# Sigmoid attention and GELU feed-forward: the seven Strassen parts of each w_out block group formed and stored in one go

## Chip, core and metric

One NeuronCore of a Trainium2 chip runs the whole program. The metric is the device time of one execution in microseconds (us). Before the change the median of three runs is 1015.89 us, from 1015.17 to 1016.56.

## What is computed

```python
scale = 1.0 / np.sqrt(q.shape[-1])
scores = scale * np.matmul(q, k.transpose(0, 1, 3, 2)) - np.log(S)
attn_out = np.matmul(1.0 / (1.0 + np.exp(-scores)), v)
x = attn_out.transpose(0, 2, 1, 3).reshape(B * S, H * D)
h = x @ w_in
g = 0.5 * h * (1.0 + erf(h / sqrt(2)))
out = g @ w_out
```

There are 8 batches of 12 heads with 448 positions of 64, so x is 3584 x 768; w_in is 768 x 2048 and w_out is 2048 x 768, both 64-bit floats.

## The kernel before

The program has two stages. **Attention** (24 units of two heads, to 242.7 us of the trace) writes x, partly into tiles and mostly to DRAM (scr_x). The **feed-forward** then runs over four blocks of two batches. Each block has a first product with w_in (`ffn1`, 56 steps) and a second with w_out (`ffn2`, 28 steps). Both use a Strassen-Winograd scheme: instead of eight block products there are seven, and the weights enter as seven parts, numbered 1 to 7. With the blocks a11, a12, a21, a22 of a weight the parts are: 1 = a11, 2 = a12, 4 = a22, 5 = s1 = a21 + a22, 6 = s2 = s1 - a11, 7 = s3 = a11 - a21, 3 = s4 = a12 - s2.

Every product is three matmuls (`terms`, L579): each operand is split in a high and a low half, and low x high, high x low and high x high are added up. So each weight tile needs a copy on ACT (the high half, `high_to`, L302) and a subtraction on DVE (the low half, `low_to`, L313), in this order.

**Weights for the feed-forward.** The class `Weights` loads tiles wst0, wst1, ... from DRAM through the SP queue, four buffers in all; ACT and DVE split tile k into whl k, again four buffers. Call this *unit k*. A unit of `ffn1` feeds two steps: unit k feeds steps 2k and 2k+1 of the list `IN_ORDER`. A step is nine matmuls of 448 columns. wst k+4 is asked for when the low half of unit k is done; the copy of unit k+4 waits until PE has used unit k. `IN_ORDER` has steps 0 to 15 for parts 1 and 2, steps 16 to 39 for parts 6, 7 and 4, the rest for 5 and 3. Part 7 goes on in the PSUM bank of part 6, and part 4 in that of part 7, so ACT must first copy out what the earlier part left: step 18 waits for the copy of step 16 (L732), step 20 for that of step 17, and step 21 (part 4) for that of step 18 (L734).

**The decoder.** The weights come as 64-bit floats. `Decoder.work` (L224) is a generator that turns them into 32-bit ones, in 28 chunks (16 of w_in, 12 of w_out): a load of about 1 MB by SP (`load`, raw, three buffers), two ACT instructions (`scale`, `place`, tile me), three DVE instructions (`join` L171 and L179, `round` L186), and then the load of the chunk three later. Two chunks make a *group*, four blocks of 128 x 512 in one tile wd (two buffers). w_out has six groups, 0 to 5. For each group the seven parts are stored to DRAM (scr_out) by DMAs that POOL issues, 256 KB each, and read back as weights later. The steps of the generator are spread over the attention units by a table and over the steps 2 to 45 of the first `ffn1` by `to`. All instructions stand on each engine in the order in which Python writes them; no scheduler moves them.

**How a group ends before the change.** `post` (L205 on) makes s1 in place of a21 (L209) and s2 (L210) in a small tile s, and stores parts 2, 4, 1, 5, 6. Some steps later `close` (L217) makes parts 3 and 7 *in place* of a12 and a22: 3 = a12 - s2 and 7 = a22 - s2 (both L220; apart from rounding the second is a11 - a21). These two must wait until the stores of a12 and a22 have read them, and only when the last two stores have landed is the wd tile free for the group two later. Group 0 gets its first part at the end of the attention, with s2 in a buffer of the ring tmp, which also holds the attention's results on their way to scr_x:

```python
            if u == total - 1:
                dec.second = lambda group: piece("s2_0")
...
                    if dec.closed < min(KE + 1, len(opened)) and n >= opened[dec.closed] + (5 if n > 3 else 3):
                        dec.close()
```

Of the kernel before, what the change touches and what calls it, by code (L numbers as in the profile page):

```python
# [8 lines left out]
F32 = mybir.dt.float32  # L9
# [6 lines left out]
ALU = mybir.AluOpType  # L16

P = 128
# [4 lines left out]
def tile_sigmoid_attention_gelu_ffn(  # L23
# [10 lines left out]
    nc = tc.nc  # L34
    B, NPAIR, _, S = q.shape
    NU = NPAIR // 2
    D = HALF
    NF, _, NC, _ = w_in.shape
# [74 lines left out]
    def piece(name):  # L113
        return sb.tile([P, QUAD], F32, tag="tmp", name=name, bufs=3)

    def square(m):
        return m.rearrange("p (h f n) -> p h f n", h=2, f=2)

    class Decoder:
        def __init__(self):  # L120
            self.raws, self.parts, self.rest, self.out = {}, {}, {}, None
            self.done = self.groups = self.closed = 0
            self.mixing, self.pending, self.open, self.second = [], [], [], None
            self.steps = self.work()
            self.taken = 0

# [64 lines left out]
            self.load(i + 3)  # L191

        def post(self):
            some = bool(self.mixing or self.pending and self.second)
            while self.mixing:
                j, a = self.mixing.pop()
                s = sb.tile([P, 2, WU], F32R, tag="whl", name=f"sin{j}", bufs=WHL)
                s = s.bitcast(F32).rearrange("p a b -> p (a b)")
                quads = [t[:, i * OP : i * OP + OP] for t in (a, s) for i in range(4)]
                parts = mix(quads[:4], quads[4:])  # L200
                for p in (1, 2, 4, 5, 6, 7, 3):
                    n = IN_ORDER.index((p, j))
                    nc.gpsimd.dma_start(scr_in[n // 2][:, n % 2], parts[p])
                self.done += 1
            while self.pending and self.second:  # L205
                (c, e), a = self.pending.pop(0)
                a11, a12, a21, a22 = (a[:, i * QUAD : i * QUAD + QUAD] for i in range(4))
                s2 = self.second(c * KE + e)
                nc.vector.tensor_tensor(a21, a21, a22, op=ALU.add)  # L209
                nc.vector.tensor_tensor(s2, a21, a11, op=ALU.subtract)  # L210
                for p, part in ((2, a12), (4, a22), (1, a11), (5, a21), (6, s2)):
                    nc.gpsimd.dma_start(scr_out[p, c][:, :, :, e], square(part))
                self.open.append((c, e, a12, a22, s2))
                self.groups += 1
            return some

        def close(self):  # L217
            c, e, a12, a22, s2 = self.open.pop(0)
            for p, part in ((3, a12), (7, a22)):
                nc.vector.tensor_tensor(part, part, s2, op=ALU.subtract)  # L220
                nc.gpsimd.dma_start(scr_out[p, c][:, :, :, e], square(part))
            self.closed += 1

        def work(self):  # L224
            for i in range(3):
                self.load(i)
            yield
            for i in range(len(CHUNKS)):
                self.scale(i)
                yield True  # L230
                self.place(i)
                yield True
                yield self.post()
                self.join(i)
                yield True
                self.round(i)
                yield True
            yield self.post()

        def go(self, steps):  # L240
            for _ in range(steps):
# [7 lines left out]
                    steps += 1  # L249

        def has(self, *need):
            return all(n >= m for n, m in zip((self.done, self.groups, self.closed), need))

        def until(self, *need):
            while not self.has(*need):
# [4 lines left out]
    LATE = 17  # L260
    STEPS = {u: (3, 2) for u in (*range(2, 10), *range(11, 19))}
    STEPS |= {20: (3, 1), 21: (4, 1), 22: (4, 1), 23: (4, 0)}
    STEPS_IN_ALL = 5 * len(CHUNKS) + 2

    class Weights:
        def __init__(self):
# [7 lines left out]
        def need(self, i):  # L274
            kind, b, u = self.units[i]
            if b > 0:
                return 0, 0, 0
            if kind == "in":
                return max(j for _, j in IN_ORDER[2 * u : 2 * u + 2]) + 1, 0, 0
            groups = KE if u[1] < KF // 4 else 2 * KE  # L280
            return KF, groups, groups if u[0] in (3, 7) else 0

        def source(self, i):
            kind, b, u = self.units[i]
# [60 lines left out]
        nc.vector.tensor_tensor(lo, src, hi, op=ALU.subtract)  # L345

    def ring(name, tag="raw"):
        n, bufs = {"raw": (RAW, 3), "me": (KC * S, 2), "wd": (4 * QUAD, 2), "s": (KC * S, 1)}[tag]
        return (late if tag == "s" else sb).tile([P, n], F32R, tag=tag, name=name, bufs=bufs)

    def braid(m):
# [12 lines left out]
    def attention(at, ps):  # L364
# [153 lines left out]
        def decode(u, place):  # L518
            if u >= total:
                return  # L520
            if u == total - 1:
                dec.second = lambda group: piece("s2_0")
            dec.go(STEPS.get(u, (0, 0))[place])

        ready = nc.const_aps.tensor(1.0, (P, S), mybir.dt.bfloat16)
# [60 lines left out]
    def feed_forward(banks):  # L586
# [110 lines left out]
        def ffn1(b, g, xs):  # L697
# [6 lines left out]
                    held[p, j] = bank()  # L704
                    nc.scalar.copy(held[p, j], g[1, 0][j // 2][:, j % 2])

            done, opened = dec.taken, []
            live = [n for n in range(2, 46) if IN_ORDER[n] not in X0_WORK]
            for n, (p, j) in enumerate(IN_ORDER):
                if n % 2 == 0:  # L710
# [38 lines left out]
                if b == 0:  # L749
                    if at in X0_WORK:  # L750
                        X0_WORK[at](xs)
                    if n in live:
                        share = (live.index(n) + 1) / len(live)
                        dec.to(math.ceil(done + (STEPS_IN_ALL - done) * share))
                    while len(opened) < dec.groups:
                        opened.append(n)
                    if dec.closed < min(KE + 1, len(opened)) and n >= opened[dec.closed] + (5 if n > 3 else 3):
                        dec.close()
                else:
                    sums = {(1, 0): 5, (1, 1): 6, (1, 2): 7, (1, 4): 4}  # L760
                    highs = {(1, 3): 6, (1, 5): 7, (1, 7): 4, (6, 3): 5, (7, 7): 3}
                    lows = {(1, 4): 6, (1, 6): 7, (2, 6): 4, (6, 4): 5, (4, 7): 3}
                    if at in sums:
                        x_sum(xs, b, sums[at])
                    if at in highs:
                        x_high(xs, b, highs[at])
                    if at in lows:
                        x_low(xs, lows[at])
# [7 lines left out]
        def ffn2(b, g):  # L776
# [19 lines left out]
            for n, (p, c) in enumerate(OUT_ORDER):  # L796
# [53 lines left out]
                if p == 6:  # L850
                    after = c == KF // 2 - 1
                    sum21 = lambda g21=g21, g12=g12: combine(g21, g21, g12)
                    later.append(sum21) if after else sum21()
                if b == 0 and n in (0, 2):
                    dec.close()
                if b + 1 < NB and n == (4 if b else 8):
                    for p, j, k in ((1, 0, 0), (8, 0, 1), (3, 1, 1), (2, 1, 0)):
                        nxt[p] = x_tile("xs", f"x{b + 1}_{j}{k}")
                        load_x(nxt[p], b + 1, j, k)
            return nxt  # L860

        def second(group):
            if group not in seconds:
                s = late.tile([P, KC * S], F32, tag="s", name=f"s2_{group}", bufs=1)
                parts = (s[:, :QUAD], s[:, QUAD : 2 * QUAD])
                seconds.update({group: parts[0], group + 1: parts[1]} if group > KE else {group: s[:, :QUAD]})
            return seconds[group]

        seconds = {}
        dec.second = second  # L870
        h2, t4 = (x_tile(f"xt{i}", f"x0_{i}") for i in range(2))
        nc.scalar.copy(h2, x0[1, 0].bitcast(F32))
        nc.scalar.activation(one, one, AF.Gelu)
# [48 lines left out]
```

## Time and profile before

| what | value |
|---|---|
| median of three runs | 1015.89 us (1015.17 to 1016.56) |
| the profiled execution, its own time | 1015.95 us |
| its span, first to last instruction | 1013.9 us |
| mean granted TensorE clock | 0.999 |
| PE busy | 1005.8 us (99%) |
| DVE busy, ACT busy, POOL busy | 704.5, 679.4, 116.1 us |
| moved by DMA | 201.22 MB |

PE is the TensorE matmul engine, DVE VectorE, ACT ScalarE, POOL GpSimd, SP the engine that issues most DMAs; "SPq" is its DMA queue. A row of the timeline gives start, duration, engine, line, operation, what it writes and reads, and in square brackets the idle time of the engine just before with what ended it. "DMA to landing" is the time from the issue of a DMA until its data are there. The profiled execution lies 0.06 us above the median.

### The profile page before, as it was taken

The numbers are of one execution on the slowest core, as the hardware profiler recorded it, in microseconds if no ns is written. First come the engines' busy times: TensorE is split into PE (matmuls) and PEld (weight loads), VectorE is DVE, ScalarE is ACT, GpSimd is POOL, SyncE is SP. The second block draws the span as 40 slices with busy tenths as digits, with TensorE's granted clock in tenths as the row PEclk, the third lists the DMA queues.
The fourth block names the chain that finished last, engine by engine and source line by source line (L and its number), as shares of the span: only waits on it lengthen the run. The fifth ranks groups of instructions, "written<-read, shape, count | busy, mean of one in ns | idle before, by whom it ended". The sixth has DMA issues, their size and how long they took to land.

```text
span 1013.9 us, 16551 instructions
## 1 busy us (share of the span) xinstructions
PE 1005.8 (99%) x6406; PEld 908.2 (90%) x6406; DVE 704.5 (69%) x822; ACT 679.4 (67%) x935; POOL 116.1 (11%) x186
## 2 busy tenths in 40 slices
PE   9999999999999999999999999999999999999998
PEld 5656666566999999999999999999999999999998
DVE  3677767787788997774378867534887774368873
ACT  5888887788887656467665655766666567665652
POOL 1342223232322210010000000100000000000000
PEclk9999999999999999999999999999999999999999
DMA  9999999997996674564344445634445543334441
GB/s 271 294 352 354 306 334 322 352 337 249 317 334 225 200 245 149 165 205 137 115 130 133 145 141 165 203 124 121 136 113 143 163 153 118 110 109 125 143 141 59
DMA packets 84141, 201.22 MB, mean 198 GB/s; under 512 B 9760, under 2 KB 34336, under 8 KB 84064
## 3 DMA queue, kind: packets, MB, share of 16 engines
q1 hardware_dynamic: 71056, 158.53, 51.2%
q0 software_dynamic: 12704, 41.30, 11.3%
q8 instruction: 50, 0.82, 0.3%
q10 hardware_dynamic: 304, 0.34, 0.1%
q14 instruction: 27, 0.22, 0.1%
HBM read 156.10 MB, written 41.29 MB: 195 GB/s over the span
## 4 chain that ended last, share of the span: by engine, by line
PE 83%; issue 8%; DMA 5%; DVE 2%; POOL 1%; ACT 1%; SPq 0%; POOLq 0%; DVEq 0%; ACTq 0%
PE pf L584 72%; PE pav L470 6%; PE sc L437 4%; DMA scr_x<-x 2%; DMA scr_in<-wd 1%; PE sc_t L454 1%; POOL scr_x L516 1%; DMA scr_out<-wd 1%; DMA wst<-scr_in 1%; DVE wd L171 1%; DVE whl L316 0%; PE warm L529 0%; ACT a L415 0%; DVE xl_p L621 0%; DMA out_dram<-tmp 0%
## 5 line engine op out<-in xcount | busy, mean ns | idle before, releaser
L584 PE MATMUL pf<-op,whl 128*128 128x448 f32 x2016 | 382.0, 352 | 0.0
L584 PEld LDWEIGHTS pf<-op,whl 128*128 128x128 f32 x2016 | 381.0, 189 | 0.3
L584 PE MATMUL pf<-xh_p,whl 128*128 128x448 f32 x1296 | 353.3, 353 | 1.5 <-ACT g L732 1.5
L309 ACT CAST whl<-wst 128x768 fp32r<-128x768 f32 x224 | 186.5, 833 | 212.9 <-PE pf L584 186.5
L316 DVE TENSOR_TENSOR whl<-wst,whl 128x768 fp32r<-128x768 f32 x224 | 213.7, 955 | 145.5 <-ACT whl L309 145.2
L584 PEld LDWEIGHTS pf<-xh_p,whl 128*128 128x128 f32 x1296 | 244.9, 189 | 3.3 <-ACT g L732 1.8
L584 PE MATMUL pf<-xl_p,whl 128*128 128x448 f32 x600 | 211.6, 353 | 1.5 <-DVE xl_p L621 1.5
L415 ACT ACTIVATE a<-sc 128x896 f32<-128x896 f32 x144 | 119.2, 935 | 35.6 <-PE sc L437 35.5
L470 PE MATMUL pav<-a,v 64*64 64x448 f32 x1296 | 133.0, 541 | 0.0
L621 DVE TENSOR_TENSOR op<-g,op 128x896 fp32r<-128x896 f32 x112 | 121.4, 1084 | 0.9 <-ACT op L631 0.9
L584 PEld LDWEIGHTS pf<-xl_p,whl 128*128 128x128 f32 x600 | 113.4, 189 | 1.9 <-DVE xl_p L621 1.8
L470 PEld LDWEIGHTS pav<-a,v 64*64 64x64 f32 x1296 | 55.4, 132 | 61.1 <-issue 33.7
L631 ACT CAST op<-g 128x896 fp32r<-128x896 f32 x112 | 104.8, 936 | 2.6 <-PE pf L584 2.6
L621 DVE TENSOR_TENSOR g<-g,g 128x896 f32<-128x896 f32 x64 | 69.4, 1084 | 0.0
L618 ACT ACTIVATE g<-tmp 128x448 f32<-128x448 f32 x64 | 40.4, 631 | 26.7 <-DVE tmp L621 26.6
L621 DVE TENSOR_TENSOR tmp<-pf,g 128x448 f32<-128x448 f32 x64 | 39.8, 623 | 26.2 <-PE pf L584 25.6
L341 POOL DMA_DIRECT2D x<-scr_x x24 | 18.0, 807 | 325.3 <-ACT g L728 219.3
L437 PE MATMUL sc<-lo,hi 64*128 64x448 f32 x276 | 51.5, 368 | 0.3 <-DVE x L508 0.3
L407 DVE TENSOR_TENSOR lo<-qk,hi 128x896 fp32r<-128x896 f32 x46 | 50.1, 1089 | 1.1
L437 PE MATMUL sc<-hi,lo 64*128 64x448 f32 x276 | 48.9, 349 | 0.0
L437 PE MATMUL sc<-hi 64*128 64x448 f32 x276 | 48.9, 349 | 0.0
L171 DVE SCALAR_TENSOR_TENSOR wd<-raw,me 128x768 uint32<-128x768 uint32 (+1 forms) x28 | 30.0, 1072 | 20.6 <-ACT me L152 11.3
(74 smaller groups left out, 773.1 us busy)
## 6 DMA issues: line engine op xcount, KB each, us to landing
wst<-scr_in SPq DMA_DIRECT2D x112, 384.0 KB, 3.2
wst<-scr_out SPq DMA_DIRECT2D x112, 384.0 KB, 3.1
v<-v_dram SPq DMA_DIRECT2D x48, 256.0 KB, 8.6
raw<-w_in_dram SPq DMA_DIRECT2D x16, 767.8 KB, 7.2
raw<-w_out_dram SPq DMA_DIRECT2D x12, 1023.5 KB, 7.8
qk<-q_dram SPq DMA_DIRECT2D x23, 448.0 KB, 10.9
qk<-k_dram SPq DMA_DIRECT2D x46, 224.0 KB, 11.4
out_dram<-tmp SPq DMA_DIRECT2D x43, 224.0 KB, 2.1
```

The costliest lines, as they stand in the source:

```text
L171: nc.vector.scalar_tensor_tensor(bits, words, 13, self.parts.pop(i), op0=ALU.logical_shift_right, op1=ALU.bitwise_or,)
L309: nc.scalar.copy(hl[:, 0], t)
L316: nc.vector.tensor_tensor(hl[:, 1], t, hl[:, 0], op=ALU.subtract)
L341: queue.dma_start(dst[:, :, a], src[:, :, a])
L407: nc.vector.tensor_tensor(lo, raw, hi, op=ALU.subtract)
L415: nc.scalar.activation(to, sc, AF.Sigmoid, bias=NEG_LOG_S, scale=SCALE)
L437: nc.tensor.matmul(sc[:, j], ks[rows(j), 1, keys], braid(qs[rows(j), 0]) if braided else qs[rows(j), 0], start=n == 0, stop=n == last,)
L470: nc.tensor.matmul(pav[rows(j), p], vals[u][half, p, j, c], a[p][half, j], start=not swap and c == order[0], stop=c == (order[-1], FULL - ...
L584: nc.tensor.matmul(bank, a, braid(m), **flags)
L618: nc.scalar.activation(straight(dst), unbraid(src), AF.Gelu)
L621: nc.vector.tensor_tensor(out, a, b, op=op)
L631: nc.scalar.copy(op[:, 0], src)
```

## The change

The two parts that were made in place, and s2, go to a tile of their own, s, with three pieces of 128 x 512 and one buffer. `post` now makes s3 (in s) and s1 (in place of a21, the only block that is still overwritten, and before it is stored) and issues the stores of parts 1, 2, 4, 5 and 7. A new step, `rest_of_group`, makes s2 and s4 in s and stores parts 6 and 3. `close`, the lists of open groups and the calls of `close` in `ffn1` and `ffn2` are gone. The tile s is allotted in the feed-forward only, so that group 0, whose blocks are ready in the attention, is mixed and stored at the start of `ffn1`; `post` takes one group at a time. The number of generator steps rises by six, so that the steps fall a little differently over `ffn1`. In numbers the four subtractions and additions of a group and its seven stores stay. Its core:

```diff
-            while self.pending and self.second:
+            if self.pending and self.third:
                 (c, e), a = self.pending.pop(0)
                 a11, a12, a21, a22 = (a[:, i * QUAD : i * QUAD + QUAD] for i in range(4))
-                s2 = self.second(c * KE + e)
+                s = self.third(c * KE + e)
+                s2, s3, s4 = (s[:, i * QUAD : i * QUAD + QUAD] for i in range(3))
+                nc.vector.tensor_tensor(s3, a11, a21, op=ALU.subtract)
                 nc.vector.tensor_tensor(a21, a21, a22, op=ALU.add)
-                nc.vector.tensor_tensor(s2, a21, a11, op=ALU.subtract)
-                for p, part in ((2, a12), (4, a22), (1, a11), (5, a21), (6, s2)):
-                    nc.gpsimd.dma_start(scr_out[p, c][:, :, :, e], square(part))
-                self.open.append((c, e, a12, a22, s2))
-                self.groups += 1
+                self.spread(c, e, ((1, a11), (2, a12), (4, a22), (5, a21), (7, s3)))
+                self.half = c, e, a11, a12, a21, s2, s4
             return some
 
-        def close(self):
-            c, e, a12, a22, s2 = self.open.pop(0)
-            for p, part in ((3, a12), (7, a22)):
-                nc.vector.tensor_tensor(part, part, s2, op=ALU.subtract)
+        def spread(self, c, e, parts):
+            for p, part in parts:
                 nc.gpsimd.dma_start(scr_out[p, c][:, :, :, e], square(part))
-            self.closed += 1
+
+        def rest_of_group(self):
+            c, e, a11, a12, s1, s2, s4 = self.half
+            self.half = None
+            nc.vector.tensor_tensor(s2, s1, a11, op=ALU.subtract)
+            nc.vector.tensor_tensor(s4, a12, s2, op=ALU.subtract)
+            self.spread(c, e, ((6, s2), (3, s4)))
+            self.groups += 1
...
                 yield self.post()
+                if self.half:
+                    self.rest_of_group()
+                    yield True
                 self.join(i)
...
-    STEPS_IN_ALL = 5 * len(CHUNKS) + 2
+    STEPS_IN_ALL = 5 * len(CHUNKS) + 2 + NO
...
-        n, bufs = {"raw": (RAW, 3), "me": (KC * S, 2), "wd": (4 * QUAD, 2), "s": (KC * S, 1)}[tag]
+        n, bufs = {"raw": (RAW, 3), "me": (KC * S, 2), "wd": (4 * QUAD, 2), "s": (3 * QUAD, 1)}[tag]
...
-            if u == total - 1:
-                dec.second = lambda group: piece("s2_0")
...
-                    while len(opened) < dec.groups:
-                        opened.append(n)
-                    if dec.closed < min(KE + 1, len(opened)) and n >= opened[dec.closed] + (5 if n > 3 else 3):
-                        dec.close()
...
-                if b == 0 and n in (0, 2):
-                    dec.close()
...
-        dec.second = second
+        dec.third = lambda group: ring(f"s_{group}", "s").bitcast(F32)
```

How instructions move on DVE between the low halves of units 7 and 9, in the first `ffn1` (whl k is unit k; wd18 and wd20 hold groups 1 and 2). Before:

```order
L316 TENSOR_TENSOR whl7_3266<-wst7_3164,whl7_3266 128x768
L171 SCALAR_TENSOR_TENSOR wd20_3263<-raw21_3061,me21_3295 128x1024
L179 TENSOR_SCALAR raw21_3061<-raw21_3061 128x1024
L316 TENSOR_TENSOR whl8_3297<-wst8_3201,whl8_3297 128x768
L186 ISA wd20_3263<-raw21_3061,wd20_3263 128x2048
L220 TENSOR_TENSOR wd18_2973<-wd18_2973,s2_1_3255 128x512 x2
L316 TENSOR_TENSOR whl9_3326<-wst9_3230,whl9_3326 128x768
L621 TENSOR_TENSOR xl0_p7_3380<-x0_01_111,xh0_p7_3361 128x1344
```

The same place in the changed program:

```order
L325 TENSOR_TENSOR whl7_3258<-wst7_3156,whl7_3258 128x768
L210 TENSOR_TENSOR s_1_3306<-wd18_2973 128x512
L211 TENSOR_TENSOR wd18_2973<-wd18_2973 128x512
L223 TENSOR_TENSOR s_1_3306<-wd18_2973 128x512
L224 TENSOR_TENSOR s_1_3306<-wd18_2973,s_1_3306 128x512
L171 SCALAR_TENSOR_TENSOR wd20_3255<-raw21_3061,me21_3277 128x1024
L179 TENSOR_SCALAR raw21_3061<-raw21_3061 128x1024
L186 ISA wd20_3255<-raw21_3061,wd20_3255 128x2048
L325 TENSOR_TENSOR whl8_3290<-wst8_3189,whl8_3290 128x768
L325 TENSOR_TENSOR whl9_3333<-wst9_3226,whl9_3333 128x768
L628 TENSOR_TENSOR xl0_p7_3382<-x0_01_111,xh0_p7_3363 128x1344
```

All of group 1's arithmetic now stands ahead of unit 8, and the chunk's L186 too. DVE from there to the low half of x for part 4 (xl0_p4, which step 21 reads), in the changed program:

```order
L210 TENSOR_TENSOR s_2_3395<-wd20_3255 128x512
L211 TENSOR_TENSOR wd20_3255<-wd20_3255 128x512
L325 TENSOR_TENSOR whl10_3365<-wst10_3261,whl10_3365 128x768
L223 TENSOR_TENSOR s_2_3395<-wd20_3255 128x512
L224 TENSOR_TENSOR s_2_3395<-wd20_3255,s_2_3395 128x512
L171 SCALAR_TENSOR_TENSOR wd22_3424<-raw22_3184,me22_3349 128x1024
L179 TENSOR_SCALAR raw22_3184<-raw22_3184 128x1024
L325 TENSOR_TENSOR whl11_3403<-wst11_3293,whl11_3403 128x768
L186 ISA wd22_3424<-raw22_3184,wd22_3424 128x2048
L628 TENSOR_TENSOR xl0_p4_3469<-x0_1_3109,xh0_p4_3437 128x1344
```

Before, the rows from xl0_p7 to xl0_p4 were the units 10 and 11, L209, L210, L171 and L179; now L223, L224 and L186 stand there as well. SP's queue before, from wst10 on:

```order
L298 DMA wst10_3269<-scr_in10_77 128x768
L133 DMA raw23_3283<-w_out_dram 128x2x2047
L298 DMA wst11_3300<-scr_in11_78 128x768
L298 DMA wst12_3329<-scr_in12_79 128x768
L133 DMA raw24_3343<-w_out_dram 128x2x2047
L298 DMA wst13_3366<-scr_in13_80 128x768
```

and in the changed program:

```order
L307 DMA wst10_3261<-scr_in10_77 128x768
L133 DMA raw23_3275<-w_out_dram 128x2x2047
L307 DMA wst11_3293<-scr_in11_78 128x768
L133 DMA raw24_3331<-w_out_dram 128x2x2047
L307 DMA wst12_3336<-scr_in12_79 128x768
L307 DMA wst13_3368<-scr_in13_80 128x768
```

The load of raw24, 1 MB, has moved ahead of that of wst12.

## Rows read from the trace of the kernel before

**Rows 1.** The page's busy time of PE and PEld: us, share, instructions.

```profile
PE 1005.8 (99%) x6406; PEld 908.2 (90%) x6406; DVE 704.5 (69%) x822; ACT 679.4 (67%) x935; POOL 116.1 (11%) x186
```

**Rows 2.** Stretches: us, busy PE, PEld, DVE, ACT, POOL, clock, DMA share, GB/s.

```profile
242.72:313.50 70.78, 67.53 (x353) 65.94 (x351) 59.37 (x65) 59.65 (x88) 20.44 (x30) 1.00 0.87 304
313.50:1007.85 694.35, 694.35 (x3671) 693.72 (x3671) 477.51 (x512) 425.50 (x615) 25.39 (x35) 1.00 0.48 146
```

**Rows 3.** Timeline of PE, the three places with idle time in the feed-forward.

```profile
248.57 1.78 PE L584 MATMUL pf<-x,whl 128*128 128x448 f32 x8 [0.28 <-DVE x L621]
...
275.73 0.46 PE L584 MATMUL pf<-xh_p,whl 128*128 128x448 f32 x1 [1.47 <-ACT g L732]
...
282.79 0.46 PE L584 MATMUL pf<-xl_p,whl 128*128 128x448 f32 x1 [1.50 <-DVE xl_p L621]
```

**Rows 4.** Timeline of DVE, the start of the feed-forward.

```profile
244.76 0.62 DVE L508 COPY x<-pav 128x448 f32<-128x448 f32 x1 [1.29 <-DMA scr_x<-x]
...
251.28 1.23 DVE L186 CUSTOM_DVE_ANT_0 wd<-raw,wd 128x2048 uint16<-128x2048 uint16 x1
...
256.83 0.68 DVE L209 TENSOR_TENSOR wd<-wd 128x512 f32<-128x512 f32 x1
257.55 0.69 DVE L210 TENSOR_TENSOR s<-wd 128x512 f32<-128x512 f32 x1
260.89 1.23 DVE L171 SCALAR_TENSOR_TENSOR wd<-raw,me 128x1024 uint32<-128x1024 uint32 x1 [2.64 <-DMA scr_out<-wd]
262.15 0.71 DVE L179 TENSOR_SCALAR raw<-raw 128x1024 uint32<-128x1024 uint32 x1
262.75 0.97 DVE L316 TENSOR_TENSOR whl<-wst,whl 128x768 fp32r<-128x768 f32 x1
263.62 1.23 DVE L186 CUSTOM_DVE_ANT_0 wd<-raw,wd 128x2048 uint16<-128x2048 uint16 x1
264.76 0.97 DVE L316 TENSOR_TENSOR whl<-wst,whl 128x768 fp32r<-128x768 f32 x1
...
267.50 0.95 DVE L316 TENSOR_TENSOR whl<-wst,whl 128x768 fp32r<-128x768 f32 x1
...
279.31 1.22 DVE L171 SCALAR_TENSOR_TENSOR wd<-raw,me 128x1024 uint32<-128x1024 uint32 x1 [3.11 <-issue]
...
281.18 1.56 DVE L621 TENSOR_TENSOR xl_p<-x,xh_p 128x1344 fp32r<-128x1344 f32 x1
```

**Rows 5.** Timeline of ACT: unit 11's copy, and the copy that step 18 needs.

```profile
273.51 0.83 ACT L309 CAST whl<-wst 128x768 fp32r<-128x768 f32 x1 [1.27 <-DMA wst<-scr_in]
...
275.14 0.54 ACT L732 COPY g<-pf 128x448 f32<-128x448 f32 x1
```

**Rows 6.** Timeline of POOL: the issue of stores.

```profile
234.87 0.54 POOL L516 DMA_DIRECT2D scr_x<-x  x1 [8.41 <-DVE x L508]
...
253.40 1.46 POOL L221 DMA_DIRECT2D scr_out<-wd  x2 [7.18 <-DVE wd L220]
...
257.81 0.71 POOL L212 DMA_DIRECT2D scr_out<-wd  x1 [0.74 <-DVE wd L209]
```

**Rows 7.** Landing of w_out stores issued around 254, 270.5, 273 and 309 us.

```profile
DMA to landing us min/median/max: 6.0/6.3/6.7
...
DMA to landing us min/median/max: 7.5/7.5/7.5
...
DMA to landing us min/median/max: 8.6/9.4/9.8
...
DMA to landing us min/median/max: 2.7/2.7/2.7
```

**Rows 8.** Timeline of SP's queue: the loads of wst12 and raw24.

```profile
268.52 0.32 SPq L298 DMA_DIRECT2D wst<-scr_in  x1
269.62 0.38 SPq L133 DMA_DIRECT2D raw<-w_out_dram  x1
```

**Rows 9.** Landing of weight loads: wst11 (issued 265.75 us), wst13 (271.69 us).

```profile
DMA to landing us min/median/max: 7.7/7.7/7.7
...
DMA to landing us min/median/max: 9.3/9.3/9.3
```

More of the change, by code (lines that the diff above doesn't have):

```diff
@@ L121, in __init__ @@
             self.raws, self.parts, self.rest, self.out = {}, {}, {}, None
-            self.done = self.groups = self.closed = 0
-            self.mixing, self.pending, self.open, self.second = [], [], [], None
+            self.done = self.groups = 0
+            self.mixing, self.pending, self.half, self.third = [], [], None, None
             self.steps = self.work()
@@ L193, in post @@
         def post(self):
-            some = bool(self.mixing or self.pending and self.second)
+            some = bool(self.mixing or self.pending and self.third)
             while self.mixing:
@@ L238, in work @@
             yield self.post()
+            self.rest_of_group()
+            yield True
         def go(self, steps):
@@ L251, in has @@
         def has(self, *need):
-            return all(n >= m for n, m in zip((self.done, self.groups, self.closed), need))
+            return all(n >= m for n, m in zip((self.done, self.groups), need))
         def until(self, *need):
@@ L276, in need @@
             if b > 0:
-                return 0, 0, 0
+                return 0, 0
             if kind == "in":
-                return max(j for _, j in IN_ORDER[2 * u : 2 * u + 2]) + 1, 0, 0
+                return max(j for _, j in IN_ORDER[2 * u : 2 * u + 2]) + 1, 0
             groups = KE if u[1] < KF // 4 else 2 * KE
-            return KF, groups, groups if u[0] in (3, 7) else 0
+            return KF, groups
         def source(self, i):
@@ L705, in begin @@
                     nc.scalar.copy(held[p, j], g[1, 0][j // 2][:, j % 2])
-            done, opened = dec.taken, []
+            done = dec.taken
             live = [n for n in range(2, 46) if IN_ORDER[n] not in X0_WORK]
@@ L860, in ffn2 @@
             return nxt
[L862 to L869, printed above, removed]
-        dec.second = second
+        dec.third = lambda group: ring(f"s_{group}", "s").bitcast(F32)
         h2, t4 = (x_tile(f"xt{i}", f"x0_{i}") for i in range(2))
```

## Prediction

> **What bounds the kernel now.** The page's first part has PE busy for 99% of the span [rows 1], so what is read next is not which engine is busiest but where PE is idle. The stretches say it: from 313.50 us to the end PE is busy for all of 694.35 us, and between 242.72 us (start of the feed-forward) and 313.50 us it is idle for 70.78 - 67.53 = 3.25 us [rows 2]. PE's timeline puts this in three places, at 248.57, 275.73 and 282.79 us [rows 3]. One matmul takes 694.35 / 3671 = 0.189 us [rows 2], a step of nine 1.70 us. Without any loss the second matmul of step 21 would come at 242.72 + 21 x 1.70 + 0.19 = 278.65 us; it comes at 282.79 us, the third idle place. So 4.1 us (the idle time and the restarts) is all that this change can win. Whatever is lost or won up to step 21 goes through to the end, as PE has no idle time behind it. A measurement of this kernel tells a difference from none at about 0.2%, 2 us.
>
> Who ends the three waits? The first, the low half of x for part 2, on DVE. The second is a copy of ACT at 275.14 us that stood behind unit 11's copy, which waited for wst11 until 273.51 us [rows 5]; wst11 had landed 7.7 us after its issue [rows 9]. The third is the low half of x for part 4, on DVE at 281.18 us. DVE's timeline tells why that is late: at 244.76 us it waits 1.29 us for a buffer of the ring tmp, at 260.89 us 2.64 us for stores of w_out that hold a wd tile, at 279.31 us 3.11 us for the next such stores (the trace names no releaser there, but the stores of 270.5 us land at 278.0 us and later) [rows 4, 7]. So DVE, in order, stands behind stores, and the low halves behind it.
>
> **What the change removes.** (1) s2 of group 0 leaves the ring tmp. The last copy of the attention then waits for the store of 234.87 us, issued long before [rows 6], and the 1.29 us go; DVE's next steps come some 1.35 us earlier (L186 at 249.9 for 251.28 us), and the first idle place of PE goes, 0.7 us with its restart. (2) Parts 3 and 7 no longer wait for stores before they are made, and wd is held by four stores that all are issued with the group. The wait at 279.31 us goes.
>
> **What it adds and moves.** Nothing is added in arithmetic or bytes: four operations of 0.69 us and seven stores a group, as before [rows 4]. Group 0's two operations and five stores move from the attention to the feed-forward, some 1.4 us of DVE. The four operations of a group now stand close together and ahead of low halves. The late pairs of `ffn2` go; DVE there hid them behind a PE that never idled [rows 2], so this is worth nothing. The larger tile s costs space alone. The new wait is s itself, one buffer: s3 of a group must wait until the three stores (7, 6, 3) of the group before have landed.
>
> I follow DVE's queue with the distances between starts in the trace: 1.26 us from L171 to L179, 0.60 to a low half, 0.87 from a low half to the next, 1.14 from L186 to a low half, 0.72 between two operations of a group [rows 4].
>
> *Group 0.* L186 249.9, unit 4 251.0, s3 251.9, s1 252.6, unit 5 253.25, x of part 6 254.1, s2 255.6, s4 256.3 to 257.0 us. POOL issues part 5 some 0.3 us after s1, at 253.6 us, and at 0.71 us each part 7, then 6 and 3 when they are made, part 3 at 257.3 us [rows 6].
>
> *First wait.* The first chunk of group 2 needs wd of group 0, so the landing of part 5. Stores took 6.0 to 9.8 us in this stretch and 2.7 us where the queues were quiet [rows 7]. I take 5.0 us, an estimate between: the raw load that these stores run against is issued 1.3 us earlier than before. L171 comes at 258.6 us, not 260.89 us. Then unit 6 260.5, L186 261.3, unit 7 262.5 to 263.4 us.
>
> *Group 1.* s3 needs part 3 of group 0: 257.3 us plus 6.5 us (the middle of the first row is 6.3 us [rows 7]) is 263.8 us. Four operations, L171 at 266.6, L179 267.8, L186 268.6, unit 8 269.7 to 270.65 us. Before, unit 8 began at 267.50 us [rows 4]. PE wants it for step 16 at 242.72 + 27.2 = 269.95 us, so PE loses 0.7 us there: what (1) had won.
>
> *Group 2.* Part 3 of group 1 is issued 3.8 us after 263.8 us, at 267.6 us: s4 ends after 2.85 us, and POOL issues four stores in a row behind s1. Meanwhile DVE does unit 9 and x of part 7, to 273.0 us, and waits. The landing takes 7.5 us (the second row, a store behind a raw load [rows 7]): 275.1 us. From there ten instructions to the low half of x for part 4, 9.0 us (two operations 1.33, unit 10 0.87, two operations 1.33, L171 1.26, L179 0.6, unit 11 0.87, L186 1.14, the low half itself 1.56): 284.1 us. PE's second matmul of step 21 then runs at 284.15 us instead of 282.79 us [rows 3], **1.4 us later**.
>
> *ACT beside it.* wst12 was loaded at 268.52 us, ahead of raw24 at 269.62 us [rows 8]. Now it waits for unit 8 (270.65 us) and stands behind 1 MB; weight loads behind a raw load took 7.7 and 9.3 us [rows 9]. With 8.5 us it lands at 279.2 us, and ACT, in order, makes the copies for steps 20 and 21 only after unit 12's (0.83 and 0.54 us [rows 5], with the handing over 1.5 us): step 20 at 280.7, second matmul of step 21 at 282.6 us. This ends before DVE's 284.1 us, but not by much; the idle place of ACT at 275.73 us is not gone, it moves to step 20.
>
> The sum: up to step 21 PE lost 4.1 us against its own pace; now it loses 284.15 - 278.65 = 5.5 us, 0.7 of it at step 16 and 4.8 at steps 20 and 21. That is +1.4 us. The profiled execution took 1015.95 us, so 1017.3 us; the median of the runs lies 0.06 us lower, which is small beside their spread. With the landings of parts 5 and 3 varied by about 0.7 us each, this case has 1015.5 to 1018.0 us as its own range.
>
> **The rivals.** *Faster: stores land quickly.* With 2.7 us, the last row [rows 7], nothing waits: L171 at 257.0, unit 8 ends at 268.6 us before it is wanted, x of part 7 ends at 270.9 us, and the low half for part 4 at 279.9 us, 2.8 us earlier than before: 1013.1 us. The limit is then DVE's own work. For it speaks that three of group 0's stores go out at 245 us, ahead of the raw load; against it that all stores between 253 and 276 us took 6.0 us or more [rows 7], with 304 GB/s moving in the whole stretch [rows 2]. The Trainium skill (DMA: Bandwidth & Descriptors, "Anatomy of one DMA") gives a DMA from the GpSimd queue a fixed 2.0 us plus its bytes at 436 GB/s; for 256 KB that would be an estimate of 2.6 us, and by it this rival would be the result. The trace agrees where the queues are quiet, 2.7 us, and not at the start of the feed-forward, 6.0 to 9.8 us [rows 7].
>
> *Slower: the one buffer of s.* If part 3 of group 1 lands as the stores of about 273 us did, after up to 9.8 us [rows 7], and part 3 of group 0 after 7.5 us, s3 of group 2 starts at 264.8 + 3.8 + 9.8 = 278.4 us and the low half for part 4 ends at 287.4 us: +4.6 us, 1020.5 us. It decides by 0.2% from a landing of 8.2 us on (267.6 + 8.2 + 9.0 = 284.8 us). For it: four stores of group 1 in a row stand behind three more and two raw loads. The load of wst12 does the same alone if it takes over 10.7 us, more than any row here.
>
> *The wait only changes its name.* DVE waits for stores of wd before and for stores of s after, ACT for wst11 before and wst12 after, and all evens out: 1015.9 us. This lies within my first case's reach and is counted with it.
>
> **The numbers.** My case with the even one: 0.55; slower 0.29; faster 0.16. Taken as results these are the chances of within 0.2%, slower and faster. The range goes from 1013.8 us, where half of the faster case is left out, to 1019.8 us, where a third of the slower one is.
>
> **What would show it.** In the changed profile PE's idle place at 248.6 us should be gone; idle places should stand near 270 us (DVE, unit 8) and 277 to 284 us (ACT and the low half for part 4), and none behind. DVE should wait for stores at L171 about 1.6 us near 258 us, and at L210 about 2 us near 275 us. wst12 should take 8 us or more. I am wrong if DVE does not wait at L210, if unit 8's low half ends before 269.9 us, or if PE idles in `ffn1` behind 290 us.

## The result, and the profile after the change

The changed kernel takes 1023.0 us (median of 6 runs, 1020.52 to 1024.87) against 1016.27 us for the kernel before beside it: ratio 1.0063 [1.0051, 1.0075], **slower by 6.7 us**. That lies above the predicted range, on the side of the slower rival. In the profiled execution of the change (1024.87 us) the feed-forward starts at 245.12 us, not at 242.72 us; a second execution of the same program has 243.40 us, so most of this is chance in the attention. I subtract 2.40 us where times of the first execution are compared with those of before.

Stretches, columns as in [rows 2]: from the start of the feed-forward to PE's last idle place, from there to 2.25 us before the end of the matmuls (as [rows 2] ends too), and three pieces at the worst place.

```profile
245.12:322.74 77.62, 70.63 (x354) 68.11 (x352) 67.46 (x74) 61.60 (x91) 28.70 (x39) 0.96 0.88 301
322.74:1017.07 694.33, 694.33 (x3670) 693.71 (x3671) 472.75 (x506) 423.48 (x613) 21.45 (x29) 1.00 0.47 143
282.00:286.00 4.00, 1.04 (x5) 1.05 (x6) 3.93 (x6) 2.36 (x5) 2.58 (x4) 0.98 0.84 278
286.00:290.00 4.00, 3.24 (x9) 2.40 (x9) 4.00 (x5) 3.50 (x5) 1.45 (x2) 0.50 0.82 243
290.00:294.00 4.00, 4.00 (x16) 3.75 (x15) 3.93 (x5) 1.62 (x3) 0.71 (x1) 0.67 0.88 294
```

As before, PE is never idle behind its last idle place [rows 2]; but the stretch ahead of it now holds 77.62 - 70.63 = 6.99 us of idle time instead of 3.25 us, and PE ran a part of it at half clock (0.50). The idle places in PE's timeline:

```profile
273.49 0.43 PE L591 MATMUL pf<-xh_p,whl 128*128 128x448 f32 x1 [0.85 <-DVE whl L325]
...
277.87 0.46 PE L591 MATMUL pf<-xh_p,whl 128*128 128x448 f32 x1 [0.74 <-ACT g L739]
...
284.96 0.46 PE L591 MATMUL pf<-xh_p,whl 128*128 128x448 f32 x1 [3.42 <-ACT g L739]
...
288.99 0.74 PE L591 MATMUL pf<-xl_p,whl 128*128 128x448 f32 x1 [0.76 <-DVE xl_p L628]
...
322.74 0.46 PE L591 MATMUL pf<-xh_p,whl 128*128 128x448 f32 x1 [1.22 <-ACT g L741]
```

The first place of [rows 3] is gone. Step 16 (273.49) waits for unit 8, step 18 (277.87, which the expectations below call step 17) and step 20 (284.96) for ACT, step 21 (288.99) for the low half of x for part 4; 322.74 us is new. DVE's timeline, which answers to [rows 4]:

```profile
252.31 1.23 DVE L186 CUSTOM_DVE_ANT_0 wd<-raw,wd 128x2048 uint16<-128x2048 uint16 x1
...
261.73 1.23 DVE L171 SCALAR_TENSOR_TENSOR wd<-raw,me 128x1024 uint32<-128x1024 uint32 x1 [2.33 <-DMA scr_out<-wd]
...
266.48 0.68 DVE L210 TENSOR_TENSOR s<-wd 128x512 f32<-128x512 f32 x1
...
272.39 1.82 DVE L325 TENSOR_TENSOR whl<-wst,whl 128x768 fp32r<-128x768 f32 x2
...
279.98 0.69 DVE L210 TENSOR_TENSOR s<-wd 128x512 f32<-128x512 f32 x1 [4.31 <-DMA scr_out<-s]
...
287.38 1.55 DVE L628 TENSOR_TENSOR xl_p<-x,xh_p 128x1344 fp32r<-128x1344 f32 x1
```

DVE still waits twice for stores: at 261.73 us for part 5 of group 0, at 279.98 us for part 3 of group 1, the reader of the one buffer of s. Group 1's first sum at 266.48 us waits for no store. ACT, in order, stands for 4.62 us in front of unit 12's copy, and step 20's copy (L739) comes behind it:

```profile
283.64 0.83 ACT L318 CAST whl<-wst 128x768 fp32r<-128x768 f32 x1 [4.62 <-DMA wst<-scr_in]
284.38 0.53 ACT L739 COPY g<-pf 128x448 f32<-128x448 f32 x1
```

Landings: part 5 of group 0 (issued 256.0 us), the stores of group 1 that began 268.2 to 270.1 us (part 3 is the last, the maximum), and wst12 (issued 273.37 us).

```profile
DMA to landing us min/median/max: 5.5/5.5/5.5
...
DMA to landing us min/median/max: 7.7/8.3/9.7
...
DMA to landing us min/median/max: 10.2/10.2/10.2
```

**Where the time went.** In this execution, from the start of the feed-forward to step 21's second matmul 40.07 us before and 43.87 us now: +3.8. From there to the last matmul's end 3.0 us more: 1.2 at 322.74, and some 1.7 behind 288.99, where nine matmuls ran at 1.2 GHz with 0.187 us more each. The second execution (1020.73 us) has the same chains with smaller sizes:

```profile
271.85 0.43 PE L591 MATMUL pf<-xh_p,whl 128*128 128x448 f32 x1 [0.94 <-DVE whl L325]
...
282.60 0.46 PE L591 MATMUL pf<-xh_p,whl 128*128 128x448 f32 x1 [3.40 <-ACT g L739]
...
318.57 0.46 PE L591 MATMUL pf<-xh_p,whl 128*128 128x448 f32 x1 [1.53 <-ACT g L741]
```

Step 20 waits for ACT there too. PE then runs at 1.2 GHz, and step 21's second matmul comes without idle time of its own, 42.78 us after the start of the feed-forward: +2.7. Behind it 1.7 us more are lost, 1.53 us of them at 318.57.

### The profile page after: what moved, and what is told of

It is laid out like the page before. It is cut to its first block, busy times and chain, and to the rows that moved or that the text cites. A ratio compares the mean times of both kernels' runs of the same rounds, so it can differ in the third digit from the quotient of the medians.

```text
span 1023.1 us, 16564 instructions
## 1 busy us (share of the span) xinstructions
PE 1010.6 (99%) x6406; PEld 911.7 (89%) x6406; DVE 706.5 (69%) x822; ACT 679.3 (66%) x935; POOL 117.1 (11%) x186
## 4 chain that ended last, share of the span: by engine, by line
PE 88%; DMA 7%; DVE 2%; ACT 2%; issue 1%; SPq 0%; POOL 0%; DVEq 0%; ACTq 0%; POOLq 0%
PE pf L591 70%; PE pav L479 10%; PE sc L446 6%; DMA qk<-k_dram 4%; DMA wst<-scr_in 2%; PE sc_t L463 1%; DMA v<-v_dram 1%; DVE whl L325 1%; DVE wd L171 1%; ACT a L424 1%; PE pav L494 0%; DMA scr_out<-wd 0%; DVE wd L186 0%; DVE xl_p L628 0%; ACT me L141 0%
## 5 line engine op out<-in xcount | busy, mean ns | idle before, releaser
L446 PEld LDWEIGHTS sc<-lo,hi 64*128 64x128 f32 x276 | 26.3, 185 | 18.1 <-issue 15.7
## 6 DMA issues: line engine op xcount, KB each, us to landing
v<-v_dram SPq DMA_DIRECT2D x48, 256.0 KB, 8.3
```

Source lines behind the costliest of these rows:

```text
L446: nc.tensor.matmul(sc[:, j], ks[rows(j), 1, keys], braid(qs[rows(j), 0]) if braided else qs[rows(j), 0], start=n == 0, stop=n == last,)
```

## The experiments

Three theories at first. **A**: two chains end close together, DVE behind the ring of s and ACT behind wst12. **B**: the ring alone. **C**: it is the *move* of group 0 into the feed-forward. **D** stands in the expectation of its run; **E**, **F**, **G** came later. All times stand in the table behind; *first product* is the time from the feed-forward's first matmul to the first matmul of `ffn2`, from PE's timeline: 99.84 us before, 106.66 and 104.22 us in two executions of the change.

### Group 1's sums in a place of their own

```diff
+            if group == 1:
+                idle = first[0, 1][3], first[1, 1][2], first[1, 1][3]
+                return [t.rearrange("p f s -> p (f s)")[:, :QUAD] for t in idle]
...
```

> Group 1's three new sums stand in parts of the first g tiles that are still idle, so that group 2's s3 waits for no store of group 1. Nothing else is changed against the changed kernel (1023.0 us). Theory A (two chains end close together: VectorE behind the ring of one s tile, and ScalarE behind unit 12's load, which stands behind a raw load in SP's queue): VectorE's 4.3 us in front of group 2's s3 goes, part 4's low half stands 4 us earlier, and step 21's 0.76 us of idle goes; but step 20 still starts at about 285, held by unit 12's load, with its 3.4 us of idle in front and the low clock behind it. So some 0.8 us faster than the changed kernel, 1022. Theory B (the ring alone costs the time): the idle at step 20 goes too, -4 us and more, 1019 or less. Theory C (it is the moved initial group, whose 2.3 us wait and 2.6 us of sums make VectorE late from its first chunk on): as A, and units 8 and 9 are still late at step 16 (0.85 us).

1021.62 us. DVE's wait at group 2's first sum went, step 21's idle too; that of step 20 behind ACT stayed (2.45 us), as A and C said, and B's 1019 did not come.

### wst12 ahead of raw24

```diff
-            self.load(i + 3)
+            if i != 21:
+                self.load(i + 3)
...
+                if i == 22:
+                    self.load(i + 2)
                 self.scale(i)
```

> Chunk 24's raw load is issued one step of the decoder later, so that unit 12's load stands ahead of it in SP's queue; nothing else is changed against the changed kernel (1023.0 us). Theory A (two chains): unit 12's load lands 1 to 4 us earlier, ScalarE's gelu is free earlier and step 20 starts at 281.5 to 283 instead of 285; but part 4's low half still stands at 289, so the idle moves to step 21 and the time stays within 1 us, 1022 to 1023. Theory B (the ring alone): the same, no change at all. A rival D (unit 12's load is the whole cause): 3.4 us of idle and the low clock go, 1018.

1022.22 us. Step 20 no longer waits, and step 21 waits 4.14 us for the low half for part 4: the idle time only moved. D falls.

### Both

> Both edits of the two kernels before together. Theory A (two chains that end close together): only now does the large idle go: step 20 and step 21 start some 3 to 4 us earlier than in the changed kernel, no idle there is over 1.5 us, and if the clock's fall to 1.2 GHz comes from the 3.4 us of idle it goes too, another 1.7 us: 1017 to 1019. If one edit alone already brought all of it (B or D), this one adds nothing to that one.

1022.76 us: **A's number did not come.** The large idle did go, and no clock fell near 286 us, but PE's idle time came back further on, and behind the last place the granted clock fell (0.50 from 320 to 322 us):

```profile
271.60 0.43 PE L593 MATMUL pf<-xh_p,whl 128*128 128x448 f32 x1 [0.80 <-ACT me L152]
276.98 0.46 PE L593 MATMUL pf<-xh_p,whl 128*128 128x448 f32 x1 [1.74 <-ACT g L741]
282.72 0.46 PE L593 MATMUL pf<-xl_p,whl 128*128 128x448 f32 x1 [0.18 <-DVE xl_p L630]
288.60 0.46 PE L593 MATMUL pf<-xh_p,whl 128*128 128x448 f32 x1 [0.60 <-ACT g L743]
302.16 0.46 PE L593 MATMUL pf<-xh_p,whl 128*128 128x448 f32 x1 [1.01 <-ACT pf L714]
318.60 0.46 PE L593 MATMUL pf<-xh_p,whl 128*128 128x448 f32 x1 [2.56 <-ACT g L743]
```

I read the two waits as symptoms of a pipeline of DVE, ACT and loads that is late as a whole; this run alone does not show it.

### Group 0 back in the attention: three places for its sums

First in a buffer of the whl ring:

```diff
+        def third_0(group):
+            s = sb.tile([P, 2, WU], F32R, tag="whl", name="s_0", bufs=WHL)
+            return s.bitcast(F32).rearrange("p a b -> p (a b)")
...
+            if u == total - 1:
+                dec.third = third_0
...
```

The attention's last unit takes one decoder step more, in which `rest_of_group` stands.

> The changed kernel with the initial group's sums and stores back in the attention's last unit (the sums in a buffer of the whl ring that is free there); the three sums in a tile of their own and the storing at once stay. Theory C (the moved initial group is what makes VectorE late): the 2.3 us wait of the first chunk of group 2 and 2.6 us of sums leave the feed-forward's front, so everything of VectorE stands 3 to 5 us earlier: units 8 and 9 are in time (no idle at step 16), group 1's s3 at 262 to 264, group 2's s3 still behind group 1's stores but at about 275 to 277, part 4's low half at about 284 to 286, and unit 12's load is issued earlier as well. Together 1016 to 1019, about the kernel before. Theory A says the same of VectorE, but if unit 12's load keeps landing 10 us after its issue, step 20 keeps an idle of about 1 us. If the time stays at 1021 or more, the moved group is not the cause, and the ring or the loads alone are.

1019.05 us, and nothing idle from 252 to 313 us, which speaks for C; but at 251.88 us PE waits 2.77 us for ACT, which waits 3.88 us to copy a unit (the trace names a store of x as what ended that wait). A pause so early is slack for everything behind it, so this run alone shows little. The next one has two buffers of v in its place (`tag="v"`):

> As the variant with the initial group back in the attention's last unit, but with its three sums in two buffers of v that are free there, since in the whl ring they kept a unit waiting for 3.9 us (2.8 us of idle at 251.9). Theory C (the moved group makes VectorE late): no idle at 251.9, the idle at steps 16 to 21 is at most 2 us in sum, since VectorE is 3 to 5 us earlier than in the changed kernel but 2.8 us less slack is given than in the variant with whl; the idle of about 2.3 us at 313 stays by theory E and by theory F. 1016 to 1018.5. If the idle up to step 21 is 4 us or more, the good result of the variant with whl came from its early idle and not from the place of the group.

1022.34 us, a miss: the attention's buffers lie where the feed-forward's first tiles are, and its first instructions waited for the stores, PE for 6.41 us at 255.14. The same happened (6.04 us, 1023.36 us, a miss as well) in a run that had this and the next edit together:

> The initial group in the attention (in buffers of v) and no steps of their own: of the change only the three sums in a tile of their own and the storing at once are left. Theories C and E together: no idle of over 0.5 us at 251.9 or at 313 to 320, at steps 16 to 21 at most 2 us, against 3.25 us of idle in the kernel before: 1013 to 1016, the kernel before or better. By theory F the late idle stays at 1 us or more: 1016 to 1018. If the tile of their own with one buffer is what costs (a group's first sum waits for the stores of the group before), VectorE waits 3 us or more at group 2 and step 21 has 3 us of idle: 1018 or more.

Its wait is the edit's own, not the change's:

```profile
252.35 1.31 ACT L874 CAST x<-x 128x1344 fp32r<-128x1344 f32 x1 [8.65 <-DMA scr_out<-s]
```

### No steps of their own

All four sums of a group are one step of the decoder, as `post` was before; group 0 stays moved.

```diff
-                if self.half:
-                    self.rest_of_group()
-                    yield True
...
                 self.half = c, e, a11, a12, a21, s2, s4
+                self.rest_of_group()
...
-    STEPS_IN_ALL = 5 * len(CHUNKS) + 2 + NO
+    STEPS_IN_ALL = 5 * len(CHUNKS) + 2
```

> The changed kernel without the six steps that it adds to the decoder: a group's four sums are one step, as the first sums were before, so that the chunks fall on the steps of the first layer on which they fell before. The initial group stays in the feed-forward. Theory E (the six steps alone push two ScalarE passes of a chunk straight in front of part 3's high half, and that is the 1.2 to 2.6 us of idle between 315 and 323 that the changed kernel and all four variants of it show): that idle is 0.3 us or less, and the idle up to step 21 stays as it was (5 to 6 us in sum), so 1021 to 1022. Theory F (the late idle is the earlier lateness carried on: ScalarE and VectorE have too much to do until 320): the late idle stays at 1 to 2.5 us, 1022 to 1024.

> The changed kernel once more, beside the others on one chip. By the account so far: 1021 to 1024; the same idle places (steps 16 and 17, 20, 21, and near 320), 6 to 7.5 us in sum; the clock at 1.2 GHz for some us behind the idle at step 20 if that idle is again over 3 us. The attention's end is not the change's doing: the feed-forward then starts at 242.5 to 245.2 by chance, as in the runs of the variants (242.7 to 245.1).

1020.79 us; the change beside it 1022.17 us, and its profiled execution is the second one above: idle places at steps 16, 20 and late, 5.87 us in sum, none at steps 18 and 21, so fewer than expected. Without the steps idle of 1.38 us is left at 276.18 and of 2.95 at 284.69 us, and none near 318 us, as E said: the added steps put L141 and L152 of a chunk straight ahead of part 3's high half. Its DVE shows what is left, the two waits for stores:

```profile
255.13 0.68 DVE L210 TENSOR_TENSOR s<-wd 128x512 f32<-128x512 f32 x1
...
260.56 1.23 DVE L171 SCALAR_TENSOR_TENSOR wd<-raw,me 128x1024 uint32<-128x1024 uint32 x1 [2.57 <-DMA scr_out<-wd]
...
265.40 0.68 DVE L210 TENSOR_TENSOR s<-wd 128x512 f32<-128x512 f32 x1
...
277.56 0.69 DVE L210 TENSOR_TENSOR s<-wd 128x512 f32<-128x512 f32 x1 [2.21 <-DMA scr_out<-s]
...
283.08 1.55 DVE L624 TENSOR_TENSOR xl_p<-x,xh_p 128x1344 fp32r<-128x1344 f32 x1
```

### Group 0 in the attention, in a buffer that nothing waits for

The same step structure, with group 0's sums in a buffer of me and a piece:

```diff
+            s = sb.tile([P, KC * S], F32, tag="me", name="s_0", bufs=2)
+            return piece("s2_0"), s[:, :QUAD], s[:, QUAD : 2 * QUAD]
...
```

> The initial group in the attention once more, without steps of their own, its sums now in a buffer of me and a piece, which are held by nothing of the feed-forward's first microseconds (in the buffers of v they held its very first instruction for 6.0 us, in the whl ring a unit for 3.9). So no idle over 0.5 us before 270. Of the change the tile of their own and the storing at once are left. Theory C with E (the moved group and the six steps make the loss): idle at steps 17 and 21 as in the kernel before, 1.5 us each or less, none near 318: 1014 to 1017. Theory G (the one tile, which a group gives back only when all three stores have landed, makes the loss): VectorE waits over 4 us at group 2's first sum, step 21 has 3 us of idle or more and the low clock behind it: 1018.5 or more.

1014.67 us, ratio 0.9991 [0.9983, 1.0000]: **the loss is gone, all of it, with the tile s of one buffer still there for groups 1 to 5.** G falls as the whole cause. Its DVE:

```profile
255.65 0.68 DVE L209 TENSOR_TENSOR s<-wd 128x512 f32<-128x512 f32 x1
...
258.43 1.22 DVE L171 SCALAR_TENSOR_TENSOR wd<-raw,me 128x1024 uint32<-128x1024 uint32 x1
...
270.87 0.69 DVE L209 TENSOR_TENSOR s<-wd 128x512 f32<-128x512 f32 x1
...
276.41 1.57 DVE L629 TENSOR_TENSOR xl_p<-x,xh_p 128x1344 fp32r<-128x1344 f32 x1
```

No wait for a store is left. The sums at 255.65 us are group 1's, where the moved version makes group 0's (255.13) and comes to group 1 only at 265.40 us. The place in the order is the same: with the move group 0 stands there, and group 1 comes one wait and some 10 us later. That group 0 also leaves the tile s here does not explain the gain, as nothing waited for its stores in s in the change (266.48 us above).

This run undoes more than the move. The kernel before made two of group 0's four sums in the attention and the other two behind L186:

```profile
252.42 1.29 DVE L220 TENSOR_TENSOR wd<-wd,s 128x512 f32<-128x512 f32 x2
```

Here all four stand in the attention. So the loss is priced against a group 0 that is wholly there, and the feed-forward has two sums and their stores less than before the change.

### The ring of s without the steps, and all three

> The changed kernel with the initial group in the feed-forward, without the six steps (1020.8 us, idle of 1.4 us at step 17 and 3.0 at step 21, clock low behind it), and with group 1's three sums in idle g tiles, so that group 2's first sum waits for no store. Theory A with E (the wait for the one tile is what is left, and with the six steps gone nothing gives it back later): idle at step 21 under 0.5 us, the clock full, none near 318; 1016 to 1018. Theory F (what is won at the front is given back later, as with the two edits together before): 1019.5 to 1021.5, with 2 us of idle or more behind 286.

1017.83 us, step 21's idle 0.61 us: with the steps gone the ring's wait is worth something (102.56 to 99.75 us of first product), but 1.03 us came back at 314.39 us, though the steps are gone. A and E hold in kind, and F in part; the intervals of this ratio and of that without the edit overlap.

> All three edits: the initial group in the attention, no steps of their own, group 1 in idle g tiles. Theories A, C and E: at most 1.5 us of idle in the whole first layer, at step 17: 1013 to 1015, faster than both kernels. Theory G: the same, since the one tile is waited for no longer. Theory F: 1016 or more.

1014.31 us, ratio 0.9998 [0.9985, 1.0011]: no better than without group 1's own place, since nothing waited for it.

### The fourth corner

> The fourth corner of the square: the initial group in the attention (sums in a buffer of me and a piece), but with the six added steps. Moved with steps was 1022.2 us (1.0064 of the kernel before), moved without them 1020.8 (1.0043), in the attention without them 1014.7 (0.9991). Theory E (the steps alone put two ScalarE passes in front of part 3's high half): an idle of 1.2 to 2.4 us near 314 and little else, so 1.5 to 2.5 us above the corner without steps, 1016 to 1017.5. If the late idle needs the lateness of the moved group (theory F), there is none, and the time is that of the corner without steps, 1014 to 1015.5.

1015.83 us, between the two numbers, with idle of 0.17 us at 279.60 and, as E said, 1.60 us in front of part 3's step. The timelines of ACT and of PE there:

```profile
306.73 1.25 ACT L141 ACTIVATE me<-raw 128x1024 f32<-128x1024 int16 x1
308.02 1.06 ACT L152 ACTIVATE me<-me 128x1024 int32<-128x1024 f32 x1
308.98 0.53 ACT L630 ACTIVATE g<-pf 128x448 f32<-128x448 f32 x1
309.40 1.30 ACT L672 CAST xh_p<-x 128x1344 fp32r<-128x1344 f32 x1
```

```profile
311.92 0.46 PE L596 MATMUL pf<-xh_p,whl 128*128 128x448 f32 x1 [1.60 <-ACT g L746]
```

But the corner without steps loses nearly as much at the start of `ffn2`, where this one loses nothing. Its PE:

```profile
345.11 5.19 PE L592 MATMUL pf<-op,whl 128*128 128x448 f32 x26 [1.40 <-DVE op L629]
```

| kernel | us | ratio to before, 95% | first product, us |
|---|---|---|---|
| the change, again | 1022.17 | 1.0064 [1.0050, 1.0079] | 104.22 |
| group 1 in its own place | 1021.62 | 1.0056 [1.0040, 1.0072] | 104.49 |
| wst12 ahead | 1022.22 | 1.0062 [1.0043, 1.0081] | 105.61 |
| both | 1022.76 | 1.0063 [1.0046, 1.0079] | 106.04 |
| group 0 in the attention, whl | 1019.05 | 1.0027 [1.0016, 1.0038] | 101.09 |
| the same, v | 1022.34 | 1.0061 [1.0048, 1.0075] | 106.63 |
| the same, v, no steps | 1023.36 | 1.0073 [1.0058, 1.0088] | 104.87 |
| no steps | 1020.79 | 1.0043 [1.0029, 1.0057] | 102.56 |
| no steps, group 1 in its own place | 1017.83 | 1.0029 [1.0019, 1.0038] | 99.75 |
| group 0 in the attention, me, no steps | 1014.67 | 0.9991 [0.9983, 1.0000] | 96.37 |
| the same, group 1 in its own place | 1014.31 | 0.9998 [0.9985, 1.0011] | 96.79 |
| group 0 in the attention, me, steps | 1015.83 | 0.9998 [0.9988, 1.0007] | 98.19 |

**The square.** The move costs 1.0064 - 0.9998 = 0.0066 with the steps and 1.0043 - 0.9991 = 0.0052 without, so 5 to 7 us. The steps cost 0.0021 with the move and 0.0007 without; the intervals overlap, so the times do not settle it, and the traces show why it is little: 1.7 to 1.8 us of first product lost, 1.0 to 1.4 us of idle saved in `ffn2`. That it is won because the last groups are made earlier is argued from the order, not shown. The sums in a tile of their own, stored at once, cost nothing that the times show; as these runs also have less of group 0 in the feed-forward than the kernel before, a small cost of the tile could be hidden.

## Why the prediction was wrong

**Right**, with 2.40 us taken off: the first idle place went; L186 at 249.91 us (249.9 predicted); step 16 lost 0.85 us (0.7); L171 came at 259.33 us (258.6, part 5's landing 5.5 for an estimated 5.0 us); DVE waits at L210, and ACT's idle place stands at step 20 behind wst12. Both chains that end at steps 20 and 21 were as told.

**Right by luck.** Group 1's first sum came at 264.08 us (263.8 predicted), but not because it waited for part 3 of group 0: that landed after 4.6 us, not 6.5 us, and the sum came straight behind unit 7, which L171 had made late. The idle place at step 18, which was to move to step 20 whole, kept 0.74 us; the later wait at step 20 hid it.

**Wrong in size.** "The landing takes 7.5 us (the second row, a store behind a raw load)": part 3 of group 1 took 9.7 us (8.6 us in the second execution), and 8.3 us was the median of the four stores that end with it. Issued at 267.7 us (predicted 267.6), it put group 2's first sum at 277.58 us instead of 275.1, and step 21 2.4 us later than forecast: +3.8 us for +1.4. "With 8.5 us it lands" was 10.2 us for wst12 (9.5 us in the second execution, where ACT's chain alone left PE idle): step 20 came at 282.56 us instead of 280.7. Part 3's landing passed the slower rival's point of decision (8.2 us), wst12's not its own (10.7 us). The slower rival told the wait rightly, with group 2's first sum at 278.4 us (277.58 measured), though it reached that partly by a landing of 7.5 us for group 0's part 3; its 1020.5 us still lacks what was lost behind step 21.

**Wrong in kind.** "As PE has no idle time behind it" was carried over from the kernel before. Behind step 21 the change lost another 3.0 us: 1.2 at the idle place of 322.74 us and 1.7 by the clock. Every run with the added steps has an idle place in front of that step (1.2 to 2.6 us); of the five without them only the one with group 1 in its own place and group 0 moved has one. The sum has a term for neither. PE idle in `ffn1` behind 290 us was one of the prediction's own signs of being wrong.

**Missed.** The move of group 0 was priced as "some 1.4 us of DVE". The square says that group 0 in the feed-forward instead of wholly in the attention is nearly the whole loss. At the attention's end DVE has room for the sums (in the changed kernel it idles 5.74 us there), and with the buffer of me the stores had landed before L171 asked for the tile. Moved, group 0 takes the place of group 1 in DVE's order, and L171 waits for its stores (2.33 us). That wait is no longer than the 2.64 us of before [rows 4]; what is new is that group 1's sums come behind it and not ahead of it (264.08 for 256.83 us), and so do its stores, for which group 2 then waits in the ring of s. The ladder carried these waits, one by one, without comparing it with a kernel in which group 0 stays. I also set the rule of the Trainium skill (DMA: Bandwidth & Descriptors, "Anatomy of one DMA"), an estimate of 2.6 us for 256 KB, against 6.0 us and more. The measurement decides: in the change the four stores of group 1 behind its sums took 7.7 us at least, but group 0's parts 6 and 3 just 4.6 us, so the 6.0 us was no floor either.

## What to carry to other kernels

Work that is moved out of a stage with room into one that an in-order engine paces can cost more than its own duration (here 5 to 7 us for four sums of 0.69 us): it takes the place of its successor, and that comes later. Before two late waits are mended one by one, look for what made both late; here, with the added steps, mending them changed nothing, and putting one group back gained 5 to 7 us. Where a wait hangs on a transfer in a loaded stretch, give the slowest row there a real chance (part 3 took 4.6 us for group 0 and 9.7 us for group 1), and test where the borrowed buffer of an experiment lies before its time is read.

## What was not expected of the hardware

TensorE's granted clock fell from 1.00 to 0.50, from 2.4 to 1.2 GHz, when PE had been idle for 3.42 us in the change (286 to 290 us), for 2.95 us in the run without steps, for 2.45 us in the one with group 1 in its own place, and for 2.56 us in the one with both edits. Stretches of the last three, in this order, columns as in [rows 2]:

```profile
286.00:288.00 2.00, 2.00 (x7) 1.81 (x6) 2.00 (x3) 1.66 (x3) 1.07 (x2) 0.50 0.69 227
```
```profile
284.00:286.00 2.00, 2.00 (x7) 1.79 (x6) 0.00 (x0) 1.97 (x4) 0.00 (x0) 0.50 1.02 406
```
```profile
320.00:322.00 2.00, 2.00 (x7) 1.79 (x6) 2.00 (x3) 0.00 (x0) 0.00 (x0) 0.50 1.04 396
```

The idle place of the run with the whl buffer, and the stretch behind it:

```profile
251.88 1.97 PE L597 MATMUL pf<-x,whl 128*128 128x448 f32 x9 [2.77 <-ACT g L741]
```
```profile
252.00:254.00 2.00, 2.00 (x11) 2.00 (x12) 1.97 (x3) 2.00 (x3) 0.00 (x0) 1.00 0.47 127
```

The clock stayed at 1.00 behind these 2.77 us, and behind 1.60 us in the last run, so the length of the idle time alone did not decide. And stores of the same 256 KB, issued between 268 and 284 us in the change, landed after 3.7 to 11.0 us while 328 GB/s were moved.
